# Attention in four-tile steps: half-row projections, half-column numerators, an order written by hand

## The chip, the cores and the metric

One core of a Trainium2 chip runs the whole program. The metric is the device time of one execution in microseconds; the median of three runs stands for the kernel. A profile of one execution goes with it. TensorE (PE in the profile) multiplies a moving operand by weights that were loaded before; VectorE (DVE), ScalarE (ACT) and GpSimd (POOL) do the rest of the arithmetic; SyncE (SP) issues most of the transfers.

## The reference

Attention with positive features, then two mixtures of experts, all in float32. Only the first part is changed:

```python
def phi(x):                                     # x: 4 x 8 x 576 x 64, w_phi: 64 x 128
    proj = np.einsum('bhsd,df->bhsf', x, w_phi)
    proj = proj - np.max(np.abs(proj), axis=-1, keepdims=True)
    return np.concatenate([np.exp(proj), np.exp(-proj)], axis=-1)   # 256 features
q_p, k_p = phi(q), phi(k)
kv  = np.einsum('bhsf,bhsd->bhfd', k_p, v)
z   = np.sum(k_p, axis=2)
num = np.einsum('bhsf,bhfd->bhsd', q_p, kv)
den = np.einsum('bhsf,bhf->bhs', q_p, z)[..., None] + 1e-06
attn = num / den                                # then transposed to 2304 tokens x 512
```

The first mixture routes each token whose `x @ w_skip` is positive to the expert of its largest logit; the second weighs all eight experts with a matrix balanced in eight rounds.

## The kernel before, in words

Eight units (two halves of the batch `bp`, four pairs of heads `hp`) of nine tiles each. A tile holds 128 rows (64 of each of the two sequences for queries; for keys, tiles 0 to 3 are one sequence, 5 to 8 the other, and tile 4 is shared in halves) and both heads side by side, 128 columns.

For each tile of keys and queries: a transpose on TensorE (`transp`, L115), split into two parts of reduced float32 (`split`, L76 on ScalarE, L79 on VectorE); projection (`proj`, L126 to L128) by a block-diagonal weight, three passes high x high, low x high, high x low; centring by the largest magnitude (`center`, L133 and L135, VectorE); two exponentials (`expo`, L144 and L145, ScalarE). Key features then meet the values with a column of ones (`kv_mm`, L180), which gives kv and z, and an identity with the gate and skip weights beside it (`augment`, L193) turns that to the side and adds nine columns of logits. Query features are transposed (`q_tr`, L212); `num` (L224) moves them, up to 320 columns, past kv as weights, and its result, with features as rows, is copied (L225) and transposed back (`finish`, L235). VectorE divides (L239 to L250) into x and into the logits. When the last head pair is done, `routed` starts the transfers of x to HBM (L1241: `xd`, `xd0`, `x2d`; 0.6 MB each) and, with the last pair of a half, `route`: a dozen small VectorE operations, an exponential, counting products on TensorE, ranks and scatters.

The order around it is the planner's: tile pools track who reads and writes, give each instruction its waits, and each engine's instructions are put in order by priority and expected times. The program only offers the work in 50 steps, with `fillers` between. The tile `x` has one buffer for both halves of the batch. The expert stage is a generator, `moe1`, that is entered from attention: `keys_done` in the last steps fetches the first expert's weights and splits two pieces a step; `last_steps` fetches the second's and transposes the first slot's rows; then two slots run whose tokens come from the first half alone, while the second half is routed.

Of the kernel before, what the change touches and what calls it, by code (L numbers as in the profile page):

```python
# [18 lines left out]
P = 128  # L19
B, H, S, DH, FH = 4, 8, 576, 64, 128  # L20
NT = 18
NJ = 9
# [16 lines left out]
def attention(tc, nc, cp, q, k, v, w_phi, w_gate, w_skip, lgs, routed, stepped, keys_done, last_steps):  # L39
# [3 lines left out]
    with ExitStack() as ctx:  # L43
        kctx = ctx.enter_context(ExitStack())
        kp = kctx.enter_context(tc.tile_pool(name="kp", bufs=2, side="right"))
        c1 = ctx.enter_context(tc.tile_pool(name="c1", bufs=1))
        wk = ctx.enter_context(tc.tile_pool(name="wk", bufs=2))
        ps = ctx.enter_context(tc.tile_pool(name="psA", bufs=2, space=PSUM))

        ident = cp["ident"]  # L50
        ws = c1.tile([P, FH], F32, name="ws")
# [3 lines left out]
        wbh = c1.tile([P, 2 * FH], F32R, name="wbh")  # L55
        wbl = c1.tile([P, 2 * FH], F32R, name="wbl")
        with tc.high_priority():
            for t in (wbh, wbl):
                nc.vector.memset(f32(t), 0.0)
        for h in range(2):  # L60
            w, wh, wl = [t[64 * h : 64 * h + 64] for t in (ws, wbh, wbl)]
            sl = slice(h * FH, h * FH + FH)
            nc.vector.tensor_copy(wh[:, sl], w)
            nc.vector.tensor_tensor(wl[:, sl], w, f32(wh)[:, sl], ALU.subtract)

        aug = kp.tile([65, H, P], F32, name="aug", bufs=1)
# [5 lines left out]
        lall = c1.tile([P, NJ, H, 9], F32, name="lall")  # L72

        def split(dst_h, dst_l, src, eng_h="act", lo=None):
            if eng_h == "act":
                nc.scalar.activation(dst_h, src, AF.Copy)  # L76
            else:
                nc.vector.tensor_copy(dst_h, src)
            (lo or nc.vector).tensor_tensor(dst_l, src, f32(dst_h), ALU.subtract)  # L79

        def load_q(bp, hp):
            t = wk.tile([P, NJ, 2, DH], F32, name="qt", tag="qt", bufs=1)
            for b in range(2):
                for h in range(2):
                    (nc.sync if bp or hp else nc.scalar).dma_start(
                        t[64 * b : 64 * b + 64, :, h],
                        q[2 * bp + b, 2 * hp + h].rearrange("(p j) d -> p j d", j=NJ),
                    )
            return t

        def load_kv(src, bp, hp, nm):
            if nm == "vt":
                t = kp.tile([P, NJ, 2, 66], F32, name=nm, tag=nm, bufs=3)
                nc.gpsimd.memset(t[:, :, :, 64:66], 1.0)
            else:
                t = kp.tile([P, NJ, 2, DH], F32, name=nm, tag=nm, bufs=1)
            for b in range(2):
                for h in range(2):
                    s = src[2 * bp + b, 2 * hp + h]
                    nc.sync.dma_start(  # L100
                        t[:, 5 * b : 5 * b + 4, h, 0:DH], s[0:512].rearrange("(p j) d -> p j d", j=4)
                    )
                s = src[2 * bp + b, 2 * hp : 2 * hp + 2, 512:576]
                nc.sync.dma_start(t[64 * b : 64 * b + 64, 4, :, 0:DH], s.rearrange("h p d -> p h d"))
            return t

        def transp(t, nm):
            pool = kp if nm == "k" else wk
            th = pool.tile([P, NJ, P], F32R, name=nm + "h", tag="Th", bufs=2)
            tl = pool.tile([P, NJ, P], F32R, name=nm + "l", tag="Tl", bufs=2)  # L110

            def group(j0, n):
                pt = ps.tile([P, 4, P], F32, name="pt", tag="T")
                for i in range(n):
                    nc.tensor.transpose(  # L115
                        pt[:, i], t[:, j0 + i].rearrange("p h d -> p (h d)"), ident
                    )
                split(th[:, j0 : j0 + n], tl[:, j0 : j0 + n], pt[:, :n])

            return th, tl, [lambda a=a: group(*a) for a in ((0, 4), (4, 4), (8, 1))]  # L120

        def proj(th, tl, j0, n):
            pp = ps.tile([P, 2, 2, FH], F32, name="pp", tag="Pj")
            for i in range(n):
                o = pp[:, i].rearrange("p h f -> p (h f)")
                nc.tensor.matmul(o, th[:, j0 + i], wbh, start=True, stop=False)  # L126
                nc.tensor.matmul(o, tl[:, j0 + i], wbh, start=False, stop=False)
                nc.tensor.matmul(o, th[:, j0 + i], wbl, start=False, stop=True)  # L128
            return pp

        def center(pp, n):
            m = wk.tile([P, 2, 2], F32, name="m", tag="m", bufs=4)
            nc.vector.tensor_reduce(m[:, :n], pp[:, :n], AX.X, ALU.max, apply_absolute_value=True)  # L133
            t = wk.tile([P, 2, 2, FH], F32, name="t", tag="t", bufs=2)
            nc.vector.tensor_tensor(  # L135
                t[:, :n], pp[:, :n], m[:, :n].unsqueeze(3).to_broadcast([P, n, 2, FH]), ALU.subtract
            )
            return t

        def expo(t, n, nm):  # L140
            f = (kp if nm == "k" else wk).tile([P, 2, 2, 2, FH], F32, name="f", tag="f", bufs=2)
            tf = t[:, :n].rearrange("p n h f -> p (n h) f")
            ff = f[:, :n].rearrange("p n h s f -> p (n h) s f")
# [4 lines left out]
        units = [(bp, hp) for bp in range(2) for hp in range(4)]  # L148
        QS = ((0, 2), (2, 2), (4, 1), (5, 2), (7, 2))
        KS = ((0, 2), (2, 2), (4, 2), (6, 2), (8, 1))  # L150
        st = {}

        def load(nm, u):
            if u < len(units):
                bp, hp = units[u]
                st[nm, u] = load_q(bp, hp) if nm == "qt" else load_kv(k if nm == "kt" else v, bp, hp, nm)

        def prep_v(u):

            st["v", u] = st.pop(("vt", u))  # L160
            load("vt", u + 1)
            st["kv", u] = wk.tile([P, 2, 2, 2, 74], F32, name="kvf", tag="kvf", bufs=2)

        def kv_mm(u, step):
            vt = st["v", u]
            j0, n = KS[step]
            f = st.pop(("f", u, step))
            for i in range(n):
                j = j0 + i
                for b in (0, 1):  # L170
                    if not (0 if b == 0 else 4) <= j <= (4 if b == 0 else 8):
                        continue
                    pr = slice(0, P) if j != 4 else slice(64 * b, 64 * b + 64)
                    first, last = (j == 0, j == 4) if b == 0 else (j == 4, j == 8)
                    for h in range(2):
                        if first:
                            st["acc", h] = ps.tile([65, 256], F32, name="kv", tag="K")
                        acc = st["acc", h]
                        r = f[pr, i, h].rearrange("p s f -> p (s f)")
                        nc.tensor.matmul(acc, vt[pr, j, h, 0:65], r, start=first, stop=last)  # L180
                    if last:
                        kvt = kp.tile([65, 2, 256], F32, name="kvt", tag="kvt")
                        for h in range(2):
                            nc.scalar.activation(kvt[:, h], st["acc", h], AF.Copy)
                        st["kvt", u, b] = kvt

        def augment(u, b):
            kvt = st.pop(("kvt", u, b))
            hp = units[u][1]
            pa = ps.tile([P, 2, 2, P], F32, name="pa", tag="N")  # L190
# [11 lines left out]
        def q_tr(u, step, f, i):  # L202
            j0, n = QS[step]
            if j0 in (0, 5) and i == 0:
                nj = 5 if j0 == 0 else 4
                st["fq"] = st["fq", u, 0 if j0 == 0 else 5] = wk.tile(
                    [P, 2, 2, 2, nj * 64], F32, name="fq", tag=f"fq{nj}", bufs=2
                )
            pt = ps.tile([P, 4, P], F32, name="ptq", tag="T")
            for h in range(2):  # L210
                for sg in range(2):
                    nc.tensor.transpose(pt[:, 2 * h + sg], f[:, i, h, sg], ident)  # L212
            jj = 64 * ((j0 + i) % 5)
            o = st["fq"][:, :, :, :, jj : jj + 64].rearrange("p h s b t -> p (h s) b t")
            nc.scalar.activation(o, pt.rearrange("p g (b t) -> p g b t", b=2), AF.Copy)
# [90 lines left out]
        for g in range(-5, 5 * (NU + 1)):  # L306
# [27 lines left out]
            if tr:  # L334
                q_tr(*tr[0])
# [953 lines left out]
```

## Time and profile before

| | us |
|---|---|
| median of 3 runs (2063.15 to 2066.62) | 2065.12 |
| the profiled execution | 2056.73 |
| its span, first to last instruction | 2055.0 |
| TensorE busy (98% of the span) | 2017.1 |
| VectorE, ScalarE, GpSimd busy | 1269.2, 935.4, 337.4 |
| mean granted TensorE clock, of full speed | 0.998 |

The busy time of TensorE counts the whole length of each instruction, and these overlap in its pipeline, so 98% says that something was always under way, not that the engine did all it can. Times in the rows are counted from the first instruction of the span. The profile calls an operation by its line, its engine and the names of the tiles that it writes and reads.

### The profile page before, as it was taken

What the parts mean: (1) busy time and instruction counts of PE and PEld (TensorE: products, weight loads), DVE (VectorE), ACT (ScalarE), POOL (GpSimd) and SP (SyncE); (2) the same over time, 40 slices, a digit from 0 to 9 for tenths busy, and PEclk for the clock granted to TensorE, in tenths of its full rate; (3) what the DMA queues carried; (4) which work ended last, traced back from release to release, by engine and by line L of the source; (5) the groups of instructions that cost most, each with busy time, mean ns of one, the idle gap of its engine ahead of it and who ended that gap; (6) DMA issues with size and microseconds to landing.
All of it is one profiled execution on the core that took longest, in us unless ns stands there. A gap on an engine that the chain in (4) does not pass through costs nothing.

```text
span 2055.0 us, 29087 instructions
## 1 busy us (share of the span) xinstructions
PE 2017.1 (98%) x10815; PEld 1769.5 (86%) x10815; DVE 1269.2 (62%) x2236; ACT 935.4 (46%) x1885; POOL 337.4 (16%) x271
## 2 busy tenths in 40 slices
PE   8999999998999999999999999999999999999999
PEld 6777778997688998988888899989988898998997
DVE  6456476775586666665745666656565666666563
ACT  5766655554544343343434434434434434444341
POOL 0001032221011122121111221221211212212210
PEclk9999999999999999999999999999999999999999
DMA  6579397665512212213122121121312221212211
GB/s 126 83 102 99 52 238 251 210 209 169 165 42 72 72 52 82 66 58 113 42 72 72 52 82 60 65 83 43 112 42 72 83 66 58 83 52 72 80 54 41
DMA packets 192532, 187.28 MB, mean 91 GB/s; under 512 B 73662, under 2 KB 148158, under 8 KB 192380
## 3 DMA queue, kind: packets, MB, share of 16 engines
q1 hardware_dynamic: 186396, 177.58, 31.6%
q0 software_dynamic: 3456, 7.09, 1.1%
q8 instruction: 87, 1.43, 0.3%
q10 hardware_dynamic: 2528, 0.66, 0.2%
q14 instruction: 65, 0.53, 0.1%
HBM read 163.70 MB, written 23.96 MB: 91 GB/s over the span
## 4 chain that ended last, share of the span: by engine, by line
PE 70%; DMA 2%; DVE 2%; ACT 1%; issue 0%; SPq 0%; ACTq 0%
PE py L1046 36%; PE pb L1010 14%; PE pd L1010 9%; PE pa L1010 9%; DMA r<-in_moe_w_dram 2%; PE pg L887 1%; PE warm L760 1%; ACT w2h L996 0%; SPq L807 0%; DVE wcl L837 0%; DVE w2l L1001 0%; PE pt L879 0%; DMA xr<-x2d 0%; DVE hl L1031 0%; ACT xch L943 0%
## 5 line engine op out<-in xcount | busy, mean ns | idle before, releaser
L1046 PE MATMUL py<-w2l,hh 128*128 128x512 f32 x1152 | 451.5, 392 | 0.0
L1046 PE MATMUL py<-w2h,hh 128*128 128x512 f32 x1152 | 451.3, 392 | 0.1
L1046 PE MATMUL py<-w2h,hl 128*128 128x512 f32 x1152 | 450.3, 391 | 0.0
L1001 DVE TENSOR_TENSOR w2l<-r,w2h 128x512 fp32r<-128x512 f32 x184 | 172.6, 943 | 211.6 <-ACT w2h L996 211.6
L1046 PEld LDWEIGHTS py<-w2l,hh 128*128 128x128 f32 x1152 | 216.1, 188 | 49.1 <-issue 0.6
L1046 PEld LDWEIGHTS py<-w2h,hl 128*128 128x128 f32 x1152 | 216.3, 188 | 37.3
L1046 PEld LDWEIGHTS py<-w2h,hh 128*128 128x128 f32 x1152 | 216.3, 188 | 36.3 <-ACT hh L1026 0.4
L1057 DVE SCALAR_TENSOR_TENSOR acc<-py,lg,acc 128x512 f32<-128x512 f32 x264 | 196.8, 746 | 68.2 <-PE py L1046 67.4
L1026 ACT ACTIVATE hh<-c 128x384 fp32r<-128x384 f32 x192 | 100.9, 525 | 211.9 <-DVE c L1086 117.5
L996 ACT ACTIVATE w2h<-r 128x512 fp32r<-128x512 f32 x184 | 114.7, 624 | 176.1 <-DMA r<-in_moe_w_dram 175.7
L839 POOL TENSOR_TENSOR r<-r,s 128x512 f32<-128x512 f32 x45 | 58.2, 1293 | 657.0 <-DVE wcl L837 645.3
L837 DVE TENSOR_TENSOR wcl<-r,wch 128x512 fp32r<-128x512 f32 x230 | 154.2, 686 | 6.6 <-ACT wch L831 6.5
L1010 PE MATMUL pb<-xch,wch 128*128 128x384 f32 x576 | 149.3, 340 | 8.5 <-ACT v L1018 6.4
L819 POOL TENSOR_TENSOR s<-r 128x512 f32<-128x512 f32 x45 | 57.9, 1288 | 582.4 <-DMA r<-in_moe_w_dram 564.0
L1010 PE MATMUL pb<-xcl,wch 128*128 128x384 f32 x576 | 147.6, 337 | 0.0
L1010 PE MATMUL pb<-xch,wcl 128*128 128x384 f32 x576 | 147.1, 336 | 0.0
L831 ACT ACTIVATE wch<-r 128x512 fp32r<-128x512 f32 x230 | 138.6, 622 | 9.8 <-PE pd L1010 3.0
L1010 PEld LDWEIGHTS pb<-xch,wch 128*128 128x128 f32 x576 | 105.0, 188 | 28.8 <-ACT v L1018 11.0
L1070 DVE TENSOR_TENSOR pb<-pb,s 128x384 f32<-128x384 f32 x96 | 54.3, 566 | 120.8 <-PE pb L1010 64.3
L1018 ACT ACTIVATE s<-pa 128x384 f32<-128x384 f32 x96 | 47.2, 492 | 174.9 <-PE pa L1010 174.9
L1031 DVE SCALAR_TENSOR_TENSOR hl<-c,hh 128x384 fp32r<-128x384 f32 x192 | 106.6, 555 | 6.9 <-ACT hh L1026 6.9
L1018 ACT ACTIVATE z<-pb 128x384 f32<-128x384 f32 x96 | 47.1, 490 | 137.9 <-PE pb L1010 137.8
(250 smaller groups left out, 3882.5 us busy)
## 6 DMA issues: line engine op xcount, KB each, us to landing
r<-in_moe_w_dram SPq DMA_DIRECT2D x168, 512.0 KB, 4.5
r<-in_moe_w_dram SPq DMA_DIRECT2D x184, 256.0 KB, 3.7
xd<-x SPq DMA_DIRECT2D x12, 576.0 KB, 13.0
x2d<-x SPq DMA_DIRECT2D x8, 576.0 KB, 14.4
xr<-x2d SPq DMA_DIRECT2D x18, 256.0 KB, 3.1
out_dram<-acc SPq DMA_DIRECT2D x18, 256.0 KB, 2.0
kt<-in_k_dram SPq DMA_DIRECT2D x32, 128.0 KB, 2.8
vt<-in_v_dram SPq DMA_DIRECT2D x32, 128.0 KB, 3.0
```

The costliest lines, as they stand in the source:

```text
L819: g.tensor_tensor(s1, a21, a22, ALU.add)
L831: nc.scalar.activation(wc[m, i][0], wsrc[m][i], AF.Copy)
L837: nc.vector.tensor_tensor(l, src[i], f32(h), ALU.subtract)
L839: (nc.gpsimd if m else nc.vector).tensor_tensor(src[3], src[2], src[6], ALU.subtract)
L996: nc.scalar.activation(h, w2r[m, b], AF.Copy)
L1001: nc.vector.tensor_tensor(l, w2r.pop((m, b)), f32(h), ALU.subtract)
L1010: nc.tensor.matmul(dst, w[:, kb, sl], x[:, kb], start=(start and m == 0), stop=(stop and m == 5), skip_group_check=True,)
L1018: nc.scalar.activation(t, src, AF.Copy)
L1026: nc.scalar.activation(hh, src, AF.Relu)
L1031: nc.vector.scalar_tensor_tensor(hl, src, 0.0, f32(hh), ALU.max, ALU.subtract)
L1046: nc.tensor.matmul(py, ht[:, i * P : i * P + P], wt, start=(m == 0), stop=(m == 11))
L1057: nc.vector.scalar_tensor_tensor(accs[t], py, lg[:, t, e : e + 1], accs[t], ALU.mult, ALU.add)
```

## The change

Attention is written anew. Tiles go by fours through one step: two pairs, each (keys or queries, two neighbouring tiles). A transpose now takes one head of two tiles, so that a half of the 128 rows is one tile's 64 dimensions. The projection is one full-float32 product per tile and head, on rows 0-63 or 64-127, into one of two banks; the splits and the block-diagonal weights are gone. The numerators take 64 columns of transposed query features as weights and move 74 columns of kv, into partitions 0-63 or 64-127; the copy and the transpose back are gone. Keys run twelve tiles ahead of queries. Inside `manual_schedule` TensorE, VectorE and ScalarE keep the order of the program; SyncE and GpSimd stay with the planner. `fillers` and the per-unit buffers go.

```diff
+        def transp(pairs):
+            pt = bank([P, G, P], "pt")
+            for i, (nm, w) in enumerate(pairs):
+                U, j = divmod(w, 2 * NJ)
                 for h in range(2):
+                    nc.tensor.transpose(
+                        pt[:, 2 * i + h], st[nm + "t", U][:, h, j : j + 2].rearrange("p j d -> p (j d)"), ident
                     )
+            th = wk.tile([P, G, P], F32, name="th", tag="th")
+            nc.scalar.activation(th, pt, AF.Copy)
...
+        def proj(th):
+            pp = ps.tile([P, 2, G, FH], F32, name="pp", tag="Pj", bufs=1)
+            for i in range(G):
+                for r in range(2):
+                    sl = slice(64 * r, 64 * r + 64)
+                    nc.tensor.matmul(
+                        pp[:, r, i], th[sl, i], ws[sl], start=True, stop=True, tile_position=(64 * r, 0)
+                    )
+            return pp
...
+        def center(pp):
+            m = wk.tile([P, 2, G], F32, name="m", tag="m", bufs=4)
+            nc.vector.tensor_reduce(m, pp, AX.X, ALU.max, apply_absolute_value=True)
+            t = wk.tile([P, 2, G, FH], F32, name="t", tag="t", bufs=1)
+            nc.vector.tensor_tensor(t, pp, m.unsqueeze(3).to_broadcast([P, 2, G, FH]), ALU.subtract)
...
+            for h in range(2):
+                for b in bs:
                     pr = slice(0, P) if j != 4 else slice(64 * b, 64 * b + 64)
+                    nc.tensor.matmul(
+                        st["acc", b][:, h],
+                        vt[pr, j, h, 0:65],
+                        f[pr, i % 2, i // 2 * 2 + h].rearrange("p s f -> p (s f)"),
...
+        def num(ws_, fq):
+            po = bank([P, 2, 2, 74], "po")
+            for i, w in enumerate(ws_):
+                kvf = st["kv", w // NJ]
+                for h in range(2):
+                    for fb in range(2):
+                        for b in range(2):
+                            nc.tensor.matmul(
+                                po[64 * b : 64 * b + 64, h, i],
+                                fq[:, i, 2 * h + fb, 64 * b : 64 * b + 64],
+                                kvf[:, b, h, fb],
+                                start=(fb == 0),
+                                stop=(fb == 1),
+                                tile_position=(0, 64 * b),
+                                skip_group_check=True,
+                            )
+            return po
...
+                if ("x", bp) not in st:
+                    st["x", bp] = c1.tile([P, NJ, D], F32, name="x", tag="x", bufs=1)
...
+        steps = []
+        for s in range(2 * NTL // G):
+            ks = [w for w in ((4 * s, 4 * s + 2) if s < 3 else (2 * s + 6,)) if w < NTL]
+            qs = [] if s < 3 else [2 * s - 6] if ks else [4 * s - NTL, 4 * s - NTL + 2]
+            steps.append([("k", w) for w in ks] + [("q", w) for w in qs])
...
+        with tc.manual_schedule(engines={nc.tensor.engine, nc.vector.engine, nc.scalar.engine}):
+            th = transp(steps[0])
+            for g in range(len(steps) + 1):
+                cur = steps[g] if g < len(steps) else []
+                nth = transp(steps[g + 1]) if g + 1 < len(steps) else None
+                if cur:
+                    t = center(proj(th))
+                th = nth
...
+                    q_tr(f, i, fqs[-1], o % 2)
+                for ub in aug_todo:
+                    augment(*ub)
+                aug_todo = []
+                f_ = expo(t) if cur else None
+                for i, w in tl["k"]:
+                    aug_todo += kv_mm(f, i, w)
+                for c in late:
+                    c()
+                late.clear()
+                if not cur:
+                    last_steps(ps)
+                for o, fq in enumerate(fqs):
+                    ws_ = [w for _, w in qs[2 * o : 2 * o + 2]]
+                    finish(ws_, num(ws_, fq))
+                f, prev = f_, cur
+                stepped()
+                if cur:
+                    early(g)
...
-            for i in range(done, min(8, done + 2) if psA is None else 8):
+            for i in range(done, min(8, done + 1) if psA is None else 8):
...
+    def early(g):
+        if g == 25 or 28 <= g < 36:
+            next(m1)
...
-            gates.extend([lambda: None] * 2 + [go])
+            gates.extend([lambda: None, rt.route2, go])
```

`late` holds the copies of finished kv sums, which so come behind the exponentials on ScalarE. `early` stands in the place of `keys_done`. Routing of the first half is cut in two, `route` and a step later `route2` (from the counting products on), and three scatters go out per step in place of two. Transfers of keys and queries take both heads at once, with the head outside, so that pieces are longer.

## Rows read from the trace of the kernel before

**Rows 1.** Stretches: us, busy and (instructions) of each engine, PEclk, DMA share, GB/s.
```profile
17.30:279.40 262.10, 260.84 (x1699) 200.38 (x1699) 143.55 (x345) 183.38 (x397) 14.02 (x18) 1.00 0.67 107
...
279.40:503.00 223.60, 213.76 (x1431) 196.52 (x1430) 157.10 (x306) 112.78 (x234) 56.49 (x51) 0.98 0.68 209
...
288.20:291.50 3.30, 3.30 (x32) 3.30 (x29) 2.75 (x13) 1.48 (x4) 0.00 (x0) 0.50 1.13 122
```

**Rows 2.** Time line of TensorE: start us, us, engine line operation out<-in.
```profile
6.33 1.08 PE L115 MATMUL pt<-ident,kt 128*128 128x128 f32 x4 [6.33 <-DMA kt<-in_k_dram]
...
17.32 1.91 PE L180 MATMUL kv<-f,vt 128*65 128x256 f32 x8 [0.28 <-issue]
...
279.44 0.74 PE L668 MATMUL ph<-xTh,w1h 128*128 128x256 f32 x4
```

**Rows 3.** Groups of TensorE by shape, 0 to 300 us: xcount | busy, mean ns.
```profile
L212 PE MATMUL ptq<-ident,f 128*128 128x128 f32 x288 | 44.7, 274 | 0.1
...
L180 PE MATMUL kv<-f,vt 128*65 128x256 f32 x256 | 62.6, 381 | 0.3 <-issue 0.3
...
L180 PE MATMUL kv<-f,vt 64*65 64x256 f32 x64 | 17.2, 389 | 0.0
...
L224 PE MATMUL pn<-fq,kvf 128*74 128x320 f32 x128 | 38.5, 434 | 0.6 <-DVE rd L240 0.4
...
L224 PE MATMUL pn<-fq,kvf 128*74 128x256 f32 x128 | 31.3, 380 | 0.4 <-DVE lall L250 0.4
...
L126 PE MATMUL pp<-wbh,kh 128*128 128x256 f32 x72 | 23.8, 333 | 0.1
...
L193 PE MATMUL pa<-aug,kvt 65*128 65x128 f32 x128 | 16.9, 275 | 0.0
...
L235 PE MATMUL po<-ident,nT 74*128 74x74 f32 x144 | 16.0, 233 | 0.1
...
L115 PE MATMUL pt<-ident,kt 128*128 128x128 f32 x72 | 13.2, 297 | 9.2 <-DMA kt<-in_k_dram 9.2
```

**Rows 4.** Time line of TensorE, two stretches of the attention stage.
```profile
21.70 0.28 PE L127 MATMUL pp<-wbh,kl 128*128 128x256 f32 x1
...
21.82 0.28 PE L128 MATMUL pp<-wbl,kh 128*128 128x256 f32 x1
...
22.03 1.08 PE L180 MATMUL kv<-f,vt 64*65 64x256 f32 x4
...
23.04 0.55 PE L115 MATMUL pt<-ident,kt 128*128 128x128 f32 x3
...
135.58 1.89 PE L180 MATMUL kv<-f,vt 128*65 128x256 f32 x8
...
145.32 0.60 PE L115 MATMUL pt<-ident,kt 128*128 128x128 f32 x4
...
145.76 0.55 PE L235 MATMUL po<-ident,nT 74*128 74x74 f32 x6
```

**Rows 5.** Groups of VectorE and ScalarE by shape, 0 to 300 us.
```profile
L133 DVE TENSOR_REDUCE m<-pp 128x4 f32<-128x512 f32 x64 | 42.9, 684 | 43.6 <-PE pp L128 43.4
...
L133 DVE TENSOR_REDUCE m<-pp 128x2 f32<-128x256 f32 x16 | 6.5, 405 | 1.7 <-PE pp L128 1.7
...
L144 ACT ACTIVATE f<-t 128x512 f32<-128x512 f32 x64 | 39.2, 625 | 22.3 <-DVE t L135 19.8 <-PE kv L180 1.8
...
L144 ACT ACTIVATE f<-t 128x256 f32<-128x256 f32 x16 | 6.7, 417 | 7.7 <-DVE t L135 4.2 <-PE kv L180 3.0
...
L510 DVE TENSOR_REDUCE ftb<-feq 128x1 f32<-128x8 f32 x2 | 0.3, 160 | 0.0
```

**Rows 6.** Time line of VectorE around x, and line 244's queue entry.
```profile
180.49 0.55 DVE L244 TENSOR_TENSOR x<-po,rd 128x384 f32<-128x384 f32 x1
...
197.57 0.56 DVE L244 TENSOR_TENSOR x<-po,rd 128x384 f32<-128x384 f32 x1 [0.99 <-DMA x2d<-x]
...
L244 DVEq EVENT_SEMAPHORE  x4: 49/50/981, 196.1 to 196.5; - x4
```

More of the change, by code (lines that the diff above doesn't have):

```diff
@@ L54, in attention @@
                 nc.scalar.dma_start(ws[64 * h : 64 * h + 64], w_phi)
[L55 to L66, printed above, removed]
+        aug = c1.tile([65, H, P], F32, name="aug")
         nc.vector.memset(aug, 0.0)
@@ L91, in load_kv, with bank, load @@
[L91 removed]
+        lall = c1.tile([P, 672], F32, name="lall")[:, 0 : NJ * H * 9].rearrange("p (j h e) -> p j h e", j=NJ, h=H)
+        def bank(shape, nm):
+            return ps.tile(shape, F32, name=nm, tag="W", bufs=4)
+        units = [(bp, hp) for bp in range(2) for hp in range(4)]
+        NU = len(units)
+        NTL = NU * NJ
+        st = {}
+        def load(nm, u):
+            if u >= NU:
+                return
+            bp, hp = units[u]
             if nm == "vt":
[L93 removed]
+                t = st[nm, u] = wk.tile([P, 1216], F32, name=nm, tag=nm, bufs=2)[:, 0 : NJ * 132].rearrange(
+                    "p (j h d) -> p j h d", j=NJ, h=2
+                )
@@ L105, in load_kv @@
-            return t
[L107 to L138, printed above, removed]
@@ L146, in expo @@
             return f
[L148 to L172, printed above, removed]
-                    pr = slice(0, P) if j != 4 else slice(64 * b, 64 * b + 64)
[L174 to L185, printed above, removed]
+        def kv_mm(f, i, w):
+            u, j = divmod(w, NJ)
+            vt = st["vt", u]
+            bs = [b for b in range(2) if 4 * b <= j <= 4 + 4 * b]
+            for b in bs:
+                if j == 4 * b:
+                    st["acc", b] = ps.tile([65, 2, 256], F32, name="kv", tag="K", bufs=2)
+            for h in range(2):
+                for b in bs:
+                    pr = slice(0, P) if j != 4 else slice(64 * b, 64 * b + 64)
+                    nc.tensor.matmul(
+                        st["acc", b][:, h],
+                        vt[pr, j, h, 0:65],
+                        f[pr, i % 2, i // 2 * 2 + h].rearrange("p s f -> p (s f)"),
+                        start=(j == 4 * b and h == 0),
+                        stop=(j == 4 * b + 4 and h == 1),
+                        skip_group_check=True,
+                    )
+            done = [(u, b) for b in bs if j == 4 * b + 4]
+            for u, b in done:
+                kvt = wk.tile([65, 2, 256], F32, name="kvt", tag="kvt")
+                st["kvt", u, b] = kvt
+                late.append(lambda kvt=kvt, acc=st["acc", b]: nc.scalar.activation(kvt, acc, AF.Copy))
+            if j == NJ - 1:
+                load("vt", u + 2)
+            return done
@@ L200, in augment, with q_tr @@
             nc.scalar.activation(st["kv", u][:, b], pa[:, :, :, 0:74], AF.Copy)
[L202 to L209, printed above, removed]
+        def q_tr(f, i, fq, o):
+            pt = bank([P, 4, P], "ptq")
```

248 lines of the change are left out of this document (88 added, 160 removed).

## The prediction

> **What bounds the kernel now.** I read the stages first, from the table of time stretches [rows 1]. Between the first key-value product and the first matrix product of the expert stage, 17.3 to 279.4 us, TensorE is busy 260.8 of 262.1 us; VectorE has 143.6 and ScalarE 183.4, and the DMA share is 0.67. So the attention stage is bound by TensorE, and an engine that gets less work there saves nothing by itself. The next stage (to 503 us) is TensorE's too, 213.8 of 223.6 us. The change touches only the first of them, so its whole effect should be how far it moves the point where the expert stage starts, 279.44 us [rows 2]. The same group shows the start: the first transpose at 6.33 us, when the first keys have landed, and the first key-value product at 17.32 us, behind transpose, projection, centring and exponentials in a chain.
>
> Then I read the groups of TensorE instructions by shape, for the counts [rows 3]. Their mean durations hold the pipeline's length, so a price per instruction has to come from a run of equal ones in the time line, (length of the run minus one mean duration) / (count minus 1) [rows 4]: the eight key-value products of 256 columns give (1.89 - 0.381)/7 = 0.216 us, the 128-column transposes (0.60 - 0.274)/3 = 0.109, the 74-column ones (0.55 - 0.233)/5 = 0.063. These instructions of full fp32 cost in proportion to their columns, whatever rows or weights they use. The split-fp32 projections of 256 columns start 0.12 apart.
>
> With these, the old stage: transposed features 288 x 0.109 = 31.4; tile transposes 144 x 0.109 = 15.7; augmenting products 128 x 0.109 = 14.0; key-value 320 x 0.216 = 69.1; numerators 128 x 0.27 (by columns) + 128 x 0.216 = 62.2; projections, six groups of 72, 432 x 0.12 = 51.8; transposes back 144 x 0.063 = 9.1. One thing more stands in [rows 4]: a group on 64 rows, at 22.03 us, begins 0.09 later after its forerunner than the 0.12 of its neighbours, and the next group on 128 rows begins 1.01 us behind it where four products need 0.86; its own first start shows as about 0.06 more (0.55 against 0.49 for three transposes). So going into the half-height array and back costs about 0.30 us. There are 16 such trips: 4.8. The sum is 258.1 us, of which 4.6 lie before 17.3 us; with 1.5 for routing and for transposes of the expert stage that stand here, 255.0 of the 262.1 us are explained. The method is good to 3%.
>
> **The change part by part.** A step now handles four tiles (two of keys, two of queries), 36 steps and a draining one.
>
> *Projection.* 36 x 8 full-fp32 products of 128 columns, two instructions each: 576 x 0.109 = 62.8 us if they follow one another, more than the 51.8 that go. But they lie in pairs on rows 0-63 and 64-127, with results in two banks. No row shows two halves at work at once (the old 64-row groups change halves only across another group), so the bounds are 62.8 and, with the second instruction of one half beside the first of the other (9 places for 16), 36 x 9 x 0.109 = 35.3. *Numerators.* The weights are now 64 columns of features and 74 columns move; the 144 transposes back disappear. 1152 x 0.063 = 72.6 in a row, 36 x 17 x 0.063 = 38.6 in pairs. *Key-value.* The same 320; the 8 shared tiles alternate halves, which saves 8 x 3 x 0.216 = 5.2 if halves overlap: 69.1 or 63.9. *Transposes, augmenting.* Unchanged, 15.7 + 31.4 + 14.0. *Array shapes.* Each step goes to half rows and back for the projection and to half columns and back for the numerators: 36 x 2 x 0.30 + 8 x 0.30 = 24.0, where 4.8 stood. For half columns no row gives the price; zero for them would save 10.8, twice would cost as much, and I take that of the rows.
>
> Sum: 222.9 us in pairs, 289.6 in a row, against 258.1. I take the pairs, because the 64-row products take the 0.216 us of the 128-row ones, so half of the array stands idle in them; but break-even lies inside. The Trainium skill speaks for it: "TensorEngine Tiling (Array Packing)", Key Properties, says that tiles load and multiply in parallel, and that a change of tiling mode drains the engine. The second half of that the 0.30 us above bear out; the first no row shows.
>
> *VectorE and ScalarE.* Centring two banks takes 684 + 2 x (684 - 405) = 1242 ns for each of two passes [rows 5], 2.5 us, and the division about 1 us: 3.5 per step. ScalarE has two exponentials of 625 + 2 x (625 - 417) = 1041 ns, three copies that I price like a 512-wide exponential, and copies of finished sums that come to some 0.5: 4.5 per step. TensorE's step is 222.9/36 = 6.2 us, so both hide, and the splits that VectorE loses were hidden already. In the hand-written order, features of a step are wanted by TensorE about one step after its projection ends, 6.2 us, and are ready after 2.5 + 2.1 + about 0.3: a slack of 1.2 us. That is the cover everything else has to fit in.
>
> *One place does not fit.* The tile x has one buffer, and the first write for the second half of the batch waits for the whole of the old x to be written to HBM: in [rows 6] the last write ends at 181.04 us, the next stands before four semaphore waits and starts at 197.57, released by x2d<-x, 16.5 us later. Now that cost 0.99 us, as the planner had put other work between. In the new order the next division comes one step (6.2 us) later, on VectorE in program order, with the routing arithmetic and the next centring queued behind it, and ScalarE's exponentials and TensorE behind those. From the old last write: 16.5 + 0.6 (division) + 8 small operations of 0.16 for routing [rows 5] + 2.5 + 2.1 = 23.0 us until TensorE has features that it wants after about 13: 10 us of stall. After such an idle time the granted clock may fall to 1.2 GHz; in [rows 1] it stands at 0.50 for 3.3 us after a thin stretch, worth 1.7. Some 21 small operations that choose the early experts, 21 x 0.16 = 3.4 us in step 25, exceed the slack by about 1.5. Together 13 us, bounds 5 (transfers landing sooner, as the key loads beside them are gone) and 17.
>
> *Loads* are fewer and longer, and hidden but for the first; I keep the start at 17.3 us, since its chain is the same. By then 3.3 us of the new work is done. Draining adds 1.5, routing and expert transposes 1.5, small waits I put at 3 (7 stood unexplained before).
>
> New start of the expert stage: 17.3 + (222.9 - 3.3) + 3 + 13 + 3 = 255.9 us, against 279.4: **23.5 us sooner**. The profiled execution took 2056.7 us (span 2055.0), 8.4 us under the median of 2065.1; the difference goes to the median: 2041.6, that is 2042 us. Expert weights are fetched earlier than before (step 25 of 36) and split one piece a step, which VectorE and ScalarE hold; the second expert's fetch still comes out at the end, as now.
>
> **The rivals.**
>
> *Halves don't overlap* (the change doesn't do what it says). All 576 + 1152 instructions queue. The step grows to 8 us, which shortens the stall on x to about 7 in all: 17.3 + (289.6 - 4.8) + 3 + 7 + 3 = 315.1, 36 us later, 2101. For it: no row shows overlap. Against it: the unused half of the array above. Between this and the forecast lie 66.7 us of pairing; below 36/(36 + 23.5) = 60% of them the kernel is slower.
>
> *Weight loads bound the numerators.* Each instruction brings its own weights for only 74 moving columns. If a load of 64 columns occupies its place for the 0.05 us by which a first product after a change of shape is late, pairs need 32 x 0.052 = 1.66 us a step, not 1.07: 21 us lost, 2063. Against it: 128-column loads follow one another every 0.063 us in the 74-column transposes [rows 4]. "TensorE: Matmul & The Clock Gate", section LDWEIGHTS, of the Trainium skill gives columns / 1.2 GHz, thus about 53 ns for 64 columns, an estimate that says the same as this rival; for 128 columns it would be 107, and the 63 ns of the trace disagree.
>
> *The gain is lost at the seam.* The second half's routing, and the second expert's weights, come after a shorter tail; each us that the first two slots don't cover comes back, up to 10: 2052.
>
> **How the numbers follow.** The forecast 0.60 (2018 to 2052: no price for half columns and a short stall below, all stalls at their upper bounds above), weight loads or an overlap in one of the two places 0.16 (2050 to 2072), no overlap 0.15 (2101), the seam 0.09 (2045 to 2060). What can be told from no change is 0.2%, 4 us. Faster: 0.58 + 0.07 + 0 + 0.07 = 0.72, in the order of the cases; same: 0.02 + 0.04 + 0 + 0.02 = 0.08; slower: 0.05 + 0.15 = 0.20. A range of 2018 to 2072 leaves out the third case and some ends.
>
> **What would show it.** The expert stage's first product (L668 before) near 256 us. In the time line, projections of the two halves starting in one place, 16 in about 1 us, and 32 numerator products in about 1.1; steps of 6 us. VectorE idle for about 10 us before a write of x, released by x2d<-x, once, near 60% of the stage, with TensorE idle behind it and a stretch at clock 0.50. Wrong would be: steps of 8 us, a stage after it that lasts longer than 223.6 us, or ScalarE as the releaser of TensorE in every step.

## The result, and the profile after

The changed kernel takes 2040.36 us, the median of four runs (2033.99 to 2044.81), against 2065.87 us (four runs, 2063.15 to 2066.68) of the kernel before on the same chip: a ratio of 0.9876, with a 95% interval from 0.9848 to 0.9905. Run again unaltered on another chip it took 2043.08 us, a ratio of 0.9878 [0.9854, 0.9901]. The time is where the prediction put it, at 2042. The traces agree less well with the sum behind it. The profiled execution of the changed kernel took 2041.64 us (span 2039.9), 15.1 us less than the profiled one of before, where the sum had 23.5. The two meet on the medians because the profiled execution of before lay 9 us under its median and that of the changed kernel 1 us over.

Nearly the whole difference stands where it was looked for. The expert stage starts at 263.04 us, 16.4 us sooner than in [rows 2], and what comes after it takes 1.3 us longer than before (2039.9 - 263.04 = 1776.9 against 2055.0 - 279.44 = 1775.6). That part is unchanged work, and in the eleven profiles of the changed kernel and its variants it lasts from 1771.0 to 1783.9 us, so 1.3 us between two single profiles is within their spread. The next fence is the table of stretches after; its columns are those of [rows 1].

```profile
17.30:86.00 68.70, 66.06 (x691) 49.84 (x688) 33.14 (x52) 42.15 (x61) 0.40 (x3) 1.00 0.65 119
86.00:89.40 3.40, 3.40 (x24) 2.84 (x23) 1.18 (x5) 0.60 (x1) 0.00 (x0) 0.51 1.10 201
89.40:159.00 69.60, 67.48 (x818) 52.94 (x816) 39.37 (x79) 42.67 (x64) 0.27 (x2) 1.00 0.90 122
159.00:175.00 16.00, 4.85 (x22) 4.29 (x21) 3.99 (x11) 4.21 (x8) 2.78 (x3) 0.57 0.64 51
175.00:186.00 11.00, 8.90 (x79) 5.93 (x79) 2.19 (x6) 2.76 (x5) 6.19 (x7) 0.84 0.04 2
186.00:257.00 71.00, 68.10 (x888) 54.96 (x886) 47.17 (x113) 50.16 (x77) 5.19 (x6) 1.00 0.63 149
262.00:485.00 223.00, 215.47 (x1473) 198.42 (x1468) 156.97 (x307) 112.51 (x234) 54.04 (x48) 0.98 0.66 203
```

The last row is the first part of the expert stage, which is unchanged (215.5 of 223 us busy, [rows 1] has 213.8 of 223.6). In the attention stage three stretches differ from the old one, in which TensorE was never short of work. From 159 to 175 us TensorE is busy 4.85 of 16 us; at 86 us and up to 186 us its granted clock is below 1.00. And its instructions are denser: 888 of TensorE in 71 us are 12.5 per us, in [rows 1] 1699 in 262.1, 6.5 per us.

The steady step, from the time line of TensorE after:

```profile
226.13 1.25 PE L205 MATMUL po<-kvf,fq 128*64 128x74 f32 x32
227.31 0.44 PE L108 MATMUL pt<-ident,kt 128*128 128x128 f32 x2
227.59 0.38 PE L108 MATMUL pt<-ident,qt 128*128 128x128 f32 x2
227.90 1.16 PE L125 MATMUL pp<-ws,th 64*128 64x128 f32 x16
228.99 1.09 PE L195 MATMUL ptq<-ident,f 128*128 128x128 f32 x8
229.92 2.04 PE L155 MATMUL kv<-f,vt 128*65 128x256 f32 x12
...
263.04 0.74 PE L613 MATMUL ph<-xTh,w1h 128*128 128x256 f32 x4
```

The counts are of instructions: the code asks for eight projections and sixteen numerator products a step, and the trace has two instructions for each. The sixteen instructions of the projections take 1.09 us from their start to the next group's, the thirty-two of the numerators 1.18 us. By [rows 4] they would take 16 x 0.109 = 1.74 and 32 x 0.063 = 2.02 us one behind the other. A plain step lasts 5.62 us from projection to projection, one with augmenting products 6.51.

The waits of TensorE in the first 300 us (engine, tile and line waited at, releaser: us in total, times, longest us):

```profile
PE ptq L195 <- DVE rk L395: 11.1, 1, 11.1
...
PE po L205 <- issue: 3.7, 2, 2.6
PE pp L125 <- DVE t L134: 2.3, 2, 1.2
PE ptq L195 <- issue: 2.0, 3, 0.9
PE pp L125 <- DVE rd L219: 1.8, 1, 1.8
```

The first row is the stall at x. Its cause stands on VectorE. The next fence has VectorE's time line, then TensorE's and ScalarE's at the same place:

```profile
150.53 0.42 DVE L228 TENSOR_TENSOR x<-po,rd 128x256 f32<-128x256 f32 x1
...
169.57 0.42 DVE L228 TENSOR_TENSOR x<-po,rd 128x256 f32<-128x256 f32 x1 [11.41 <-DMA xd<-gate]
169.91 0.18 DVE L234 TENSOR_TENSOR lall<-po,rd 128x36 f32<-128x36 f32 x1
170.01 0.22 DVE L395 TENSOR_TENSOR rk<-pr,ebase 128x72 f32<-128x72 f32 x1
...
171.22 1.22 DVE L132 TENSOR_REDUCE m<-pp 128x8 f32<-128x1024 f32 x1
172.54 1.23 DVE L134 TENSOR_TENSOR t<-pp,m 128x1024 f32<-128x1024 f32 x1
...
157.93 1.16 PE L125 MATMUL pp<-ws,th 64*128 64x128 f32 x16 [1.03 <-DVE t L134]
170.24 1.94 PE L195 MATMUL ptq<-ident,f 128*128 128x128 f32 x8 [11.15 <-DVE rk L395]
...
158.94 1.04 ACT L142 ACTIVATE f<-t 128x1024 f32<-128x1024 f32 x1
```

The first write of the second half's x waits 11.41 us, and the routing operations and the centring stand behind it. TensorE's next work, the transposes of query features, is released by the first of those routing operations; the features that they read were ready when ScalarE's exponential of 158.94 us ended, at 159.98. The releaser named for the write is a transfer of gates, which landed last; that there is a wait at all belongs to the tile x, as the run without it shows (below). Its length may be in part the gates': by the pieces in the trace, the last of x passes at 166.94 us, the last of the gates at 168.78, and the write starts 2.63 us after x's last piece, where before it started 0.86 us after. No run took the gates away.

A wait that no step of the prediction had is the second row, on "issue": TensorE waits for nothing that the profile shows, in the middle of the numerators, where no other engine's result is wanted. The time line there:

```profile
81.96 1.00 PE L205 MATMUL po<-kvf,fq 128*64 128x74 f32 x24
85.55 0.48 PE L205 MATMUL po<-kvf,fq 128*64 128x74 f32 x8 [2.59 <-issue]
85.96 0.65 PE L108 MATMUL pt<-ident,kt 128*128 128x128 f32 x2
...
86.96 2.08 PE L125 MATMUL pp<-ws,th 64*128 64x128 f32 x16
```

After the 2.59 us the granted clock is 0.51 for 3.4 us (second row of the stretches), and the same sixteen projections take 2.08 instead of 1.16 us. The same happens, more briefly, near 141 us (1.09 us). "Wait for instructions" below is a reading of these waits; no row shows an instruction missing.

### The profile page after: what moved, and what is told of

It reads as the page before. It is cut to its first block, busy times and chain, and to the rows that moved or that the text cites. A ratio compares the mean times of both kernels' runs of the same rounds, so it can differ in the third digit from the quotient of the medians.

```text
span 2039.9 us, 30601 instructions
## 1 busy us (share of the span) xinstructions
PE 1979.4 (97%) x11711; PEld 1743.2 (85%) x11711; DVE 1258.9 (62%) x2150; ACT 898.1 (44%) x1705; POOL 336.5 (16%) x271
## 4 chain that ended last, share of the span: by engine, by line
PE 70%; DMA 3%; DVE 2%; ACT 1%; SPq 0%; issue 0%; ACTq 0%
PE py L991 36%; PE pb L955 14%; PE pd L955 9%; PE pa L955 9%; DMA r<-in_moe_w_dram 3%; PE pg L832 1%; PE warm L705 1%; DVE wcl L782 0%; SPq L752 0%; DMA xr<-x2d 0%; ACT w2h L941 0%; PE pt L824 0%; DVE hl L976 0%; ACT xch L888 0%; DVE c L1043 0%
## 5 line engine op out<-in xcount | busy, mean ns | idle before, releaser
L946 DVE TENSOR_TENSOR w2l<-r,w2h 128x512 fp32r<-128x512 f32 x184 | 177.2, 969 | 207.1 <-ACT w2h L941 207.0
```

What stands on the lines that cost most here:

```text
L946: nc.vector.tensor_tensor(l, w2r.pop((m, b)), f32(h), ALU.subtract)
```

## The experiments

Each kernel is the changed kernel with the edit shown. The three on the halves and the one with four tiles for x ran on one chip beside the kernel before (2069.45 us, 21 runs); the one with the transposes moved, the unaltered one, the spaced one and the combination on another (2067.32, 9 runs); the two on issuing queues on a third (2065.98, 7 runs). So ratios to before are what is compared across them. "First expert product" is the start of the expert stage in the profiled execution, 263.04 us in the changed kernel.

**Do the halves run at once?** Three kernels keep every instruction and change only which half follows which. In the cuts, `...` stands for code left out.

```
# e1: projection, all of the one row half ahead of the other
-            for i in range(G):
-                for r in range(2):
+            for r in range(2):
+                for i in range(G):
# e2: numerators, all of the one column half ahead of the other
-            for i, w in enumerate(ws_):
-                ...
-                        for b in range(2):
+            for b in range(2):
+                for i, w in enumerate(ws_):
# e12: both
```

> Same products, but a step's eight projections on rows 0-63 come first and the eight on rows 64-127 after them, so that neighbours share a half. Theory (neighbours in different halves run side by side): 16 instructions take 16 x 0.109 = 1.74 us in place of 1.09, 0.65 us a step, 36 steps, 23 us: about 2063 us. Rival (the halves never overlapped, the gain came from the missing transposes back and the shorter order): no change, 2040 us within 5.

Measured: 2064.78 us (10 runs), ratio 0.9976 [0.9950, 1.0003]. Plain steps of 6.16 us, 0.54 more than 5.62; first expert product at 287.02 us.

> Same products, but the numerators of columns 0-63 come first in a step and those of columns 64-127 after them. Theory (side by side): 32 x 0.063 = 2.0 us in place of 1.19, 0.8 us a step, 36 pairs, 30 us: about 2070. Rival 1 (no overlap before): no change. Rival 2 (the weight loads bound the numerators, 0.052 us each): 1.66 us a pair already before, so 12 us at most, 2052.

Measured: 2071.11 us (10 runs), ratio 1.0001 [0.9981, 1.0021]. Plain steps of 6.44 us, 0.82 more; first expert product at 288.57 us.

> Both orders at once. Theory: 23 + 30 = 53 us, less some 3 us by which longer steps shorten the one stall on x: about 2090 us, which is slower than the kernel before the change by about 25 us; so the pairing alone would decide the sign. Rival (only one of the two overlaps): 2063 or 2070. Rival (none): 2040.

Measured: 2083.91 us (6 runs), ratio 1.0067 [1.0042, 1.0091], slower than before. Plain steps of 6.99 us, 1.37 more; first expert product at 303.21 us. Its plain step, in TensorE's time line:

```profile
244.56 1.71 PE L125 MATMUL pp<-ws,th 64*128 64x128 f32 x16
246.20 1.09 PE L195 MATMUL ptq<-ident,f 128*128 128x128 f32 x8
247.13 1.89 PE L155 MATMUL kv<-f,vt 128*65 128x256 f32 x8
248.95 2.08 PE L205 MATMUL po<-kvf,fq 128*64 128x74 f32 x32
250.96 0.44 PE L108 MATMUL pt<-ident,kt 128*128 128x128 f32 x2
```

The same sixteen instructions of the projections take 1.64 us instead of 1.09, the same thirty-two of the numerators 2.01 instead of 1.18, and nothing else in the step moves. So neighbours on different halves overlap, in both places, and the order of the loops alone is worth 36 x 1.37 = 49 us of TensorE's time; 40 of them reach the first expert product (303.21 - 263.04). Without it the change is a loss. The 3 us that the stall at x was to lose by longer steps did not come (TensorE idles 12.7 us there, 11.1 in the changed kernel); what shrank are the waits on "issue" in the numerators, to 1.1 us in all from 3.7. The rival of weight loads falls too: it wanted 1.66 us for the pairs of a step (1.92 by the 0.06 us that the prediction read for a first start), and they take 1.18. The Trainium skill, "TensorE: Matmul & The Clock Gate", section LDWEIGHTS, gives columns / 1.2 GHz for a load, by which an estimate for 64 columns is 53 ns. Here each numerator instruction brings its own load, and 32 of them take 1.18 us, 37 ns each, so the measurement decides against that figure as a bound in pairs.

**What does a change of the array's shape cost?** The projection of a step is put right behind the numerators of the one before, the next step's transposes after it. That makes three changes of shape per step out of four (half columns, half rows, full) and moves no other work.

```
-                nth = transp(steps[g + 1]) if g + 1 < len(steps) else None
                 t = center(proj(th))
                 ...
-                th = nth
+                th = transp(steps[g + 1]) if g + 1 < len(steps) else None
```

> The next step's four transposes come behind the projection in place of ahead of it, so that half columns are followed by half rows with no full-array work between: three changes of shape a step for four. Theory (each change drains the array and shows the first load, 0.15 us): 36 x 0.15 = 5 us less, about 2035. Rival (a change from half columns to half rows costs as much as the two it replaces): no change.

Measured: 2035.93 us (5 runs, 2034.72 to 2039.99), ratio 0.9843 [0.9820, 0.9867]; the changed kernel beside it 2043.08 (2041.20 to 2049.31). First expert product at 257.81 us, 5.2 to 5.9 us sooner than in the two profiles of the changed kernel. From the time line:

```profile
232.00 1.26 PE L205 MATMUL po<-kvf,fq 128*64 128x74 f32 x32
233.19 1.16 PE L125 MATMUL pp<-ws,th 64*128 64x128 f32 x16
234.28 0.66 PE L108 MATMUL pt<-ident,qt 128*128 128x128 f32 x4
234.77 1.04 PE L195 MATMUL ptq<-ident,f 128*128 128x128 f32 x8
...
238.65 1.16 PE L125 MATMUL pp<-ws,th 64*128 64x128 f32 x16
```

The step from 233.19 to 238.65 is 5.46 us long, 0.15 less than 5.62. Steps of the other kinds lose the same 0.15 (6.36 for 6.51, 5.75 for 5.91). The four transposes here take 0.49 us to the next start; in the changed kernel, where they stand between two changes, 0.59; the query transposes behind them lose the other 0.05 (0.88 for 0.93). So the change of shape that was taken out cost 0.15 us, half of the 0.30 that the prediction read for a trip there and back. The numerators take as long ahead of half rows (1.19) as ahead of the full array (1.18). What half columns cost by themselves is not isolated by this run: it lies within that 1.18.

**Is the stall the tile x, and is it worth 10 us?** x becomes four tiles, one for each pair of heads, so that no write waits for another pair's transfers.

```
-                if ("x", bp) not in st:
-                    st["x", bp] = c1.tile([P, NJ, D], F32, name="x", tag="x", bufs=1)
+                if ("x", u) not in st:
+                    st["x", u] = c1.tile([P, NJ, P], F32, name="x", tag=f"x{hp}", bufs=1)
...
-            go = lambda t=t: nc.sync.dma_start(t[:, :, sl], x[:, :, sl])
+            go = lambda t=t: nc.sync.dma_start(t[:, :, sl], x)
```

> x is four tiles, one per head pair, of the same size in all, so that the second half's first write waits for a transfer of three units earlier only. Theory (the wait for the whole of x held VectorE for 11.4 us and TensorE for 11.2, and the low clock after it cost some 4): no wait of VectorE on a transfer of x, no TensorE idle of over 3 us between 150 and 190 us, clock 1.0 there, 15 to 20 us less than the changed kernel: 2020 to 2026. Rival (routing and its small operations are next in line and hold VectorE as long, since they sit in the same place): 3 us or less, 2037.

Measured: 2039.03 us (4 runs, 2029.77 to 2043.52), ratio 0.9839 [0.9795, 0.9883]. The wait on x is gone: step 23, 19.89 us long before, takes 7.41, and TensorE's time line from 159 to 172 us has no long idle time. But the first expert product comes at 260.04 us, only 3 us sooner: the expectation is missed. What grew is the wait on "issue"; its row in the waits of TensorE in this kernel:

```profile
PE po L205 <- issue: 7.2, 2, 4.0
```

It stands at the same two places, 3.96 us near 82 and 3.27 near 143, and steps 11, 12 and 20 take 10.54, 8.40 and 10.36 us instead of 5.62, 6.51 and 5.62. That forms the theory of the next runs: TensorE runs out of instructions when the three transfers of an x, in pieces of 512 bytes, occupy the DMA queues. For it: TensorE stops at the same place each time, with 24 of the 32 numerator instructions of step 11 done, pieces of 16,384 bytes on the instruction queue pass at about that time (one at 83.2 us in the changed kernel), and in the 16 us before it the 512-byte pieces slow down from 27 ns to a mean of up to 187 ns (in stretches of 2 us).

**The changed kernel once more**, to have it beside the next kernels.

> The changed kernel unaltered, beside the others of this call. 2033 to 2045 us; TensorE starved for 1 to 4 us near 83 and 141 us, at an instruction fetch that begins late while x goes out, and for 11 us near 159.

Measured: 2043.08 us (5 runs, 2041.20 to 2049.31), the stall of instructions 2.87 us near 82 us, the stall at x 10.64, first expert product at 263.75. So these two stalls belong to the kernel, not to one execution. The shorter wait near 141 us does not: here all 32 numerator instructions run through from 141.30 us, and that part of the expectation is missed.

**Is it the burst of x's transfers?** As the kernel with four tiles, but of the three transfers of each x only the first leaves at once; the second and third are issued one and two steps later, from ScalarE's queue.

```
...
+            elif i:
+                spaced.extend([lambda: None] * (i == 1) + [lambda go=go: go(e=nc.scalar)])
             else:
                 go()
...
     # and in stepped(), once a step:
+        if spaced:
+            spaced.pop(0)()
```

> x in four tiles as in e3, and of each x the first transfer goes out as before, the second a step later and the third two steps later, from ScalarE's queue, whose order is the program's. Theory (the three transfers at once fill the DMA queues for 15 to 18 us, and TensorE's instructions come through the same queues, too late for a stream that is now denser): no TensorE idle for lack of instructions of over 1 us before 200 us, clock 1.0 from 21 us to the end of the stage; against e3 and against the changed kernel some 15 us less, about 2022. Rival 1 (the fetch is late for another reason): the idle places at 83 and 143 us stay, 2035 or more. Rival 2 (issuing from ScalarE blocks it): ScalarE becomes TensorE's releaser in those steps, 2040.

Measured: 2029.59 us (5 runs, 2025.97 to 2031.02), ratio 0.9808 [0.9784, 0.9832]; first expert product at 251.23 us. Steps 11, 12 and 20 have their plain lengths (5.61, 6.51, 5.61). TensorE's time line where the stall was:

```profile
80.81 1.89 PE L155 MATMUL kv<-f,vt 128*65 128x256 f32 x8
82.63 1.25 PE L205 MATMUL po<-kvf,fq 128*64 128x74 f32 x32
...
84.40 1.16 PE L125 MATMUL pp<-ws,th 64*128 64x128 f32 x16
```

All 32 numerator instructions run through. It missed the expected 2022 by 7.6 us, and one disturbance of that size is left: step 24 takes 12.98 us, 7.4 over its plain length, with idle times for instructions inside the projection itself, while two postponed transfers and nine scatters of the routing are under way:

```profile
162.40 0.39 PE L125 MATMUL pp<-ws,th 64*128 64x128 f32 x2 [0.32 <-issue]
163.11 0.38 PE L125 MATMUL pp<-ws,th 64*128 64x128 f32 x2 [0.32 <-issue]
164.53 0.50 PE L125 MATMUL pp<-ws,th 64*128 64x128 f32 x4 [1.04 <-issue]
166.65 1.31 PE L125 MATMUL pp<-ws,th 64*128 64x128 f32 x5 [1.62 <-issue]
```

**The time of issue, or the other queue?** That edit changed both. Two kernels change one each: all three transfers at once, two of them from ScalarE's queue; and spaced, but all from SyncE's.

```
# e9, from e3
-            go = lambda t=t: nc.sync.dma_start(t[:, :, sl], x)
+            go = lambda t=t, e=nc.scalar if i else nc.sync: e.dma_start(t[:, :, sl], x)
# e10, from e6
-                ... [lambda go=go: go(e=nc.scalar)]
+                ... [lambda go=go: go()]
```

> x in four tiles; the three transfers of each x issued at once as in the changed kernel, but the second and third from ScalarE's queue. It parts the two things that the spaced version changed together: the time of issue and the issuing queue. Theory (what counts is how many 512-byte pieces are outstanding when TensorE's next instructions are to be fetched): the stalls inside the numerators near 82 and 143 us stay, 2 us or more together, steps 11, 12 and 20 longer than 5.6, 6.5 and 5.6; about 2037 to 2043 us. Rival (it was the queue of SyncE that held the fetch back): no idle time of TensorE for instructions at these two places, and about 2030 us.

Measured: 2033.38 us (4 runs), ratio 0.9847 [0.9831, 0.9864]; first expert product at 256.73. The stall stays, 2.06 us behind 23 numerator instructions; steps 11, 12 and 20 take 7.89, 8.11 and 7.54 us. There is a wait of 1.86 us near 141 as well, ahead of the numerators, but the trace puts it down to ScalarE (f, L141, which had ended 0.9 us before) and not to "issue", so it can't be counted as the same.

> As the spaced version (x in four tiles, second and third transfer of each x one and two steps later), but all from SyncE's queue. Theory (spacing is what helps): steps 11, 12 and 20 at their plain lengths of 5.6, 6.5 and 5.6 us, no idle time for instructions near 82 and 143 us, about 2030 us. Rival (the other queue is what helped): the stalls of 2 to 4 us come back, about 2039 us.

Measured: 2029.37 us (4 runs, 2026.14 to 2040.41), ratio 0.9837 [0.9804, 0.9871]; first expert product at 255.00. The stall stays (3.14 and 1.91 us), which looks like the rival's outcome until SyncE's time line is read. The transfers of the pair before the stall leave so in this kernel:

```profile
67.39 1.37 SPq L1198 DMA_DIRECT2D xd<-x  x2
68.81 1.02 SPq L1198 DMA_DIRECT2D x2d<-x  x1
73.15 9.58 SPq L99 DMA_DIRECT2D qt<-in_q_dram  x4
```

In the spaced kernel the first leaves SyncE at 66.63 us, and the other two leave from ScalarE's queue:

```profile
66.63 0.58 SPq L1198 DMA_DIRECT2D xd<-x  x1
...
70.18 0.57 ACTq L1198 DMA_DIRECT2D xd<-x  x1
76.08 0.54 ACTq L1198 DMA_DIRECT2D x2d<-x  x1
```

SyncE has nothing to wait for between them, so the three leave within 2.5 us in spite of their new places in the program: this kernel spaced nothing and repeats the one with four tiles. ScalarE issues in order behind its own exponentials, so there the transfers do leave 3.6 and 9.5 us after the first. Of the two reasons the queue is ruled out by the first of these kernels: at once from two queues stalls like at once from one, and up to the last x that kernel differs from the spaced one only in the time of these two issues. Every profile with the three at once and plain steps of 5.5 to 5.6 us has the stall (2.06 to 3.96 us near 80 us); the spaced kernel has none, and its combination with the moved transposes, below, 0.89 us. With longer steps the three at once cost 3.00 and 2.92 us there (plain steps of 6.16 and 6.44 us) and 0.54 us (6.99 us).

By the medians the four-tile kernels can't be told apart (the intervals of 0.9808, 0.9837, 0.9839 and 0.9847 overlap), so what the spacing is worth rests on the traces: 4 to 9 us at the first expert product.

**Both edits that helped, together:** spaced transfers and transposes behind the projection.

> e6 with the order of e4. By the theories of both: 5 us below e6, about 2017. By the rivals: as e6.

Measured: 2024.89 us (5 runs, 2021.04 to 2030.35), ratio 0.9795 [0.9767, 0.9823]; first expert product at 244.65 us, step 24 still 11.86. The expected 2017 is missed, as it was worked out from 2022 for the spaced kernel. The gain over the spaced kernel agrees with what the transposes were to bring: 4.7 us by the medians, which are not apart by their intervals, and 6.6 us at the first expert product. The changed kernel on the same chip it beats by 18 us.

## Why the prediction was right, and where it was not

*The bound.* Right. TensorE bounds the stage after as before, the start moved 16.4 us, and what follows neither gave back nor added more than 1.3 us; the rival of the seam did not come, as far as single profiles can tell.

*Pairs.* Right, with the sizes a little off. Undoing both costs 49 us where the sum had 27.5 + 34.0 = 61.5 for these two places: 36 x 0.55 = 20 for the projection, 36 x 0.83 = 30 for the numerators. The break-even that the prediction named lay inside: the kernel without pairs is slower than before, though at 2084 and not 2101.

*Shapes.* Right in the sum: 0.15 us for the change that was taken out; half columns were not measured by themselves. In the plain step everything beyond the columns' own time, pairs included, comes to 0.15 + 1.09 + 0.06 + 0.09 + 1.18 = 2.57 us; the sum had 0.98 + 1.07 + 0.60 = 2.65.

*VectorE and ScalarE.* Right in the steady steps: neither releases TensorE there, and the two centring passes take 1.22 and 1.23 us (1242 ns forecast).

*The place at x.* That VectorE would be held at the write of x, and TensorE behind it, was right. The path from there to TensorE was not, and that the idle time agrees, 11.15 us where 10 were forecast, is luck. The sum let TensorE run on for about 13 us after the last write of the old x and then wait until 23.0 for features, behind division, routing, centring and exponentials. In the trace that write ends at 150.95 us; TensorE stops 8.1 us later, at 159.09, and goes on 19.3 us later, at 170.24. What it wants there are not new features, which it has from 159.98 us on, but that VectorE reads a result: the profile names the routing operation L395, two operations behind the held write. `bank` hands out four buffers in turn, so one that VectorE had not read yet is the likely reason; the rows name only the operation. Two errors of 4 to 5 us cancel.

That longer steps shorten this wait, as the rival of no overlap had it (to about 7 us), did not come either: 12.7 us with plain steps of 6.99 us. And the term of 13 us for all that goes with the wait was mis-sized. Steps 22 to 27 take 58.67 us where steps 13 to 18, the same kinds nine steps earlier, take 35.93: 22.7. Beside the 11.2 these are about 3.8 at a granted clock of 0.5 (half of the 4.6 us from 170.2 us on and of 3.1 us around 183; forecast 1.7), 2.1 in three waits for instructions at 179 to 183 us (not forecast), 1.0 before the projection of step 23 and 1.8 for the division behind the choice of the early experts (1.5 forecast); 2.8 were not attributed, of which the counting products of the routing, in step 22, are 0.5.

*What no step had.* The waits for instructions near 83 and 141 us, with the half clock after the first: steps 11, 12 and 20 cost 5.8 us more than their plain lengths. The old stage had 6.5 instructions a us and no such wait; that twice the density made TensorE's instructions something that can be late is argued, and the wait of only 0.54 us in the kernel with both orders apart, whose steps are the longest, goes with it. The Trainium skill, "Runtime: NRT & Kernel Launch", section Instruction fetch mechanics, says that a sequencer fetches its next 16 KiB block over a DMA queue of its own while it runs the present one, and that this is mostly hidden. The pieces of 16,384 bytes on the queue that the profile calls instruction agree with the first part. If the waits are for instructions, "hidden" does not hold here, where TensorE stood for 2.06 to 3.96 us in runs with three transfers of x at once.

The start of the expert stage can be put together from these: forecast 255.9, 9.7 more at x, 5.8 at the stalls, 0.5 at the start, and 8.9 less in the rest, where mean steps of 6.09 us (28 to 33) stand against 6.19 and fewer small waits than were put aside; that is 263.0. Two errors of opposite sign were hidden in the total, and the 9 us by which before's profiled execution was quicker than its median hid what was left of them, so that the hit at 2042 is in part luck. That difference stays open: the runs cannot say in which stage a typical run of before is slower than the profiled one. The two profiles of the changed kernel, 7.7 us apart, differ by 0.7 us at the start of the expert stage and by 7.0 behind it.

Open as well is the way in which x's transfers delay the instructions. In the changed kernel the 16,384-byte piece passes from 83.2 to 84.2 us and TensorE resumes at 85.55; in the kernel with the second queue the piece had passed by 82.6 and TensorE resumed at 86.22. So the late start of that piece is not the whole of it. Nor is the slowness of x's pieces: in the spaced kernel, which has no stall, their mean reaches 193 ns in 2 us (187 in the changed kernel), and an instruction piece passes from 80.2 to 82.4 us. No run took the scatters near 160 us away, so that they cause the last disturbance is only argued.

## What to carry to other kernels

Products on half the rows or half the columns of the array are worth having when neighbours alternate halves: the order of the inner loop decided here between 1.2% faster and 0.7% slower, and each change of shape wants 0.15 us in the sum. When work is repacked into more and smaller TensorE instructions, look in the trace for "issue" waits inside a group that waits for no result, and keep large bursts of small-piece transfers apart in time, by an engine that is held up by its own work; a later place in the program of an engine with nothing to wait for moves nothing. And a difference between two single profiled executions should be set against where each lies among its kernel's runs before it is moved to a median.

## What the hardware showed that was not expected

- Three transfers of 576 KB in pieces of 512 bytes, issued together, were followed some 17 us later by 2.06 to 3.96 us in which TensorE waited for nothing that the profile shows (six profiles with plain steps of 5.5 to 5.6 us). With the second and third issued 3.6 and 9.5 us after the first there was no such wait, and with 3.0 and 8.7 us, in the last kernel, one of 0.89 us.
- A wait of 2.59 us was followed by a granted clock of 0.51 for 3.4 us, in which the sixteen instructions of the projections took 2.08 instead of 1.16 us: it cost about 1.1 us on top in the following step.
- Two gate transfers in pieces of 4 bytes kept SyncE's queue 11.01 us in issuing, behind x's transfers; the same two took 1.58 us before, where the loads of keys stood between:

```profile
150.98 1.34 SPq L1192 DMA_DIRECT2D xd<-x  x2
152.37 2.23 SPq L1192 DMA_DIRECT2D x2d<-x  x1
154.69 11.01 SPq L1178 DMA_DIRECT2D xd<-gate  x2
```
